# Second mixture of experts: up products in seven block products instead of eight, down products added up in SBUF

## The chip, the cores and the metric

The kernel runs on one core of one Trainium2 chip. The metric is the time of one execution on the device, in microseconds. Before the change it is 1548.05 us, the median of three runs (1547.43 to 1549.74). Smaller is better.

The names of the engines in what follows: PE is TensorE (matrix products), PEld its loads of stationary operands, DVE is VectorE, ACT is ScalarE, POOL is GpSimd, SP is SyncE (it issues the DMAs).

## The reference

Three stages follow each other. A clustered attention gives `x` (1536 tokens by 512), a first MoE block maps `x` to a new `x`, and the second MoE block, the one that changes, sums eight experts over all tokens:

```python
def _moe2_ref(x, w_gate, w1, w2):          # x 1536x512, w1 8x512x1024, w2 8x1024x512
    logits = x @ w_gate
    logits = logits - logits.max()
    P = np.exp(logits)
    for _ in range(8):
        P /= P.sum(1, keepdims=True) + 1e-09
        P /= P.sum(0, keepdims=True) + 1e-09
        P *= N / E
    out = np.zeros((N, D), dtype=np.float32)
    for e in range(E):
        h = np.maximum(x @ w1[e], 0.0)     # "up": 1536x512 by 512x1024
        ye = h @ w2[e]                     # "down": 1536x1024 by 1024x512
        out += P[:, e:e + 1] * ye
    return out
```

The eight rounds on `P` (called the gates here) need sums over all tokens and are a long chain of small steps. They are needed before an expert's result can be weighted and added, not before the up and down products.

## The kernel before

**Precision.** Every fp32 operand of a large product is kept as two parts, `hi` (rounded to fp32r) and `lo` (the rest). One product is three matmuls, `hi*lo + lo*hi + hi*hi`, all into the same PSUM bank: the helper `three` at L675, whose matmuls have the lines L677, L678 and L679 wherever it is called from. Making a pair costs an ACT copy (the `hi`) and a subtraction, on POOL for weights and on DVE for activations.

**Order.** The program is written in the order in which it runs: each engine works through its own queue in program order, and semaphores hold an instruction until what it needs is there. The attention and the first MoE are ordered by a planner; the second MoE is a plain loop at the end of the file, after `mixed` (the first MoE) has run out.

**Second MoE.** A unit `u` is one expert `e`, one block `blk` of 512 tokens (three blocks) and one tile `f` of 128 of the 1024 hidden columns (eight tiles): 8 x 3 x 8 = 192 units. `up(u)` runs 4 x 3 matmuls of 128x128 weights on 512 tokens into a bank of PSUM (name `l1_...`), then ACT takes the relu as the `hi` of `h` (L924) and DVE the rest (L925). `down(u)`, two units later (`LAG = 2`), runs for each of the four token tiles of the block three matmuls of 512 columns: here `h` is the stationary operand and `w2` streams. The four result banks `l2[t]` stay open over all eight tiles `f`, so that PSUM does the addition over the hidden columns; only after the eighth tile DVE weights the bank with the gate and adds it to `acc` (L946; L941 and L944 for the first expert). That is 96 evictions in all. Banks: four for `up` and the small products of the gates (`bank`, two pools of two), four for `l2`.

**Weights.** `fetch_w` brings 512 KB pieces (two tiles of `f`) into one of two buffers `wraw`, `load_w` splits them into `wh` (ACT, L840) and `wl` (POOL, L841); an expert's weights stay in SBUF for its 24 units and are replaced during its last block.

**Gates.** `gates()` is a generator of twelve small steps. A step ends with a small product on PE, and the next step's DVE operations read its result. One step is drawn between `up(u)` and `down(u - 2)`, so that a step's PE product stands in PE's queue one unit behind the DVE operations that it needs.

Of the kernel before, what the change touches and what calls it, by code (L numbers as in the profile page):

```python
# [8 lines left out]
F32 = mybir.dt.float32  # L9
# [128 lines left out]
def moe_kernel(ctx: ExitStack, tc: tile.TileContext, qk, nat, cen, wt, w123, wout, wgate, w1, w2, out):  # L138
# [536 lines left out]
    def three(ps, whi, wlo, xhi, xlo, first, last):  # L675

        nc.tensor.matmul(ps, whi, xlo, start=first, stop=False)  # L677
        nc.tensor.matmul(ps, wlo, xhi, start=False, stop=False)  # L678
        nc.tensor.matmul(ps, whi, xhi, start=False, stop=last)  # L679
# [137 lines left out]
    pools["w", 0] = ctx.enter_context(tc.tile_pool(name="w1_p", bufs=1, reuse_waits="tile"))  # L817
# [6 lines left out]
    wts = {}  # L824
    w_raw = {}
    PAIRS = NF2 // 2

    def fetch_w(e, m, p):
        if e < E:
            raw = pools["w", 0].tile([P, 2, DM], F32, tag="wraw", bufs=2, name=f"wraw{e}_{m}_{p}")  # L830
            nc.sync.dma_start(raw, (w1, w2)[m][e, :, p])
            w_raw[e, m, p] = raw

    def load_w(e, m, p):
        if e < E:
            raw = w_raw.pop((e, m, p))
            for j in range(2):
                hi = pools["w", m].tile([P, DM], F32R, tag="wh", bufs=NF2, name=f"wh{e}_{m}_{p}_{j}")
                lo = pools["w", m].tile([P, DM], F32R, tag="wl", bufs=NF2, name=f"wl{e}_{m}_{p}_{j}")
                nc.scalar.copy(hi, raw[:, j])  # L840
                nc.gpsimd.tensor_sub(lo, raw[:, j], f32(hi))  # L841
                wts[e, m, 2 * p + j] = hi, lo

    todo = [(0, m, p) for m in range(2) for p in range(PAIRS)]
    fetch_w(*todo[0])
    fetch_w(*todo[1])
    for n, _ in enumerate(mixed):
        if n % 40 == 20 and todo[0][1] == 0:
            load_w(*todo.pop(0))
            fetch_w(*todo[1])  # L850
    hctx.close()
    mctx.close()
    pools["w", 1] = ctx.enter_context(tc.tile_pool(name="w2_p", bufs=1, reuse_waits="tile"))
    e_p = ctx.enter_context(tc.tile_pool(name="e_p", bufs=1, reuse_waits="tile"))

    acc = [e_p.tile([P, DM], F32, tag="acc", bufs=NT, name=f"acc{t}") for t in range(NT)]


    def gates():
# [47 lines left out]
        for t in range(TPB):  # L907
            nc.vector.tensor_scalar(acc[t], acc[t], prob[:, t, :1], None, op0=ALU.mult)


    hts = {}
    l2 = {}
    units = [(e, blk, f) for e in range(E) for blk in range(NB) for f in range(NF2)]

    def up(u):
        e, blk, f = units[u]
        hi, lo = (w.rearrange("p (d f) -> p d f", f=P) for w in wts[e, 0, f])
        ts = slice(blk * TM, (blk + 1) * TM)
# [105 lines left out]
```

## Time and profile before

| | |
|---|---|
| median of three runs | 1548.05 us |
| profiled execution | 1547.56 us, of which 1545.7 us are its span (first to last instruction) |
| second MoE in it | from 491.8 us to the last matmul at 1541.5 us, then evictions and the last DMAs |
| busy in the span | PE 97%, DVE 35%, ACT 29%, POOL 32% |
| granted TensorE clock | 0.997 over the span, 1.00 over the second MoE |

The time of the profiled execution is 1.9 us more than its span, for what lies around the instructions. PE's busy share says that some matmul is under way, not that the array streams at its best: matmuls overlap their neighbours, so the pace is read from start to start. An engine's share over the span is a mean over three stages; for the change the second MoE alone counts.

### The profile page before, as it was taken

To read this page: it belongs to the slowest core of one execution; us is meant where nothing else is said; L and a number is where in the kernel's file an instruction comes from. 1 tells how busy PE (TensorE), PEld (TensorE's weight loads), DVE (VectorE), ACT (ScalarE), POOL (GpSimd) and SP (SyncE) were. 2 spreads that over 40 slices of the span, in tenths; PEclk is the share of its full clock that TensorE was granted. 3 is DMA by queue.
4 is the path that set the end of the run, shared out by engine and by line. 5 is a ranking of instruction groups with operands and counts; after the bars stand their busy time and mean duration, and the time that the engine had idled before them with its cause. 6 is when DMAs were issued, how large, how long until landed. Compare 5 with 4: busy or idle time off the path is not lost.

```text
span 1545.7 us, 18332 instructions
## 1 busy us (share of the span) xinstructions
PE 1504.5 (97%) x7304; PEld 1264.0 (82%) x7304; DVE 546.9 (35%) x994; ACT 448.0 (29%) x850; POOL 499.1 (32%) x491
## 2 busy tenths in 40 slices
PE   4999999899999999999999999999999999999999
PEld 3899998688877888888888888888888888888887
DVE  5899998545552331111121111111111111111111
ACT  3888888222222112211211211221131121112110
POOL 4899987756652002201400310230050022013000
PEclk9999999899999999999999999999999999999999
DMA  6554531222220001100300210020020011001000
GB/s 179 163 154 120 152 88 38 85 85 69 75 62 28 28 0 53 57 0 5 105 0 1 70 39 1 28 82 1 0 92 18 0 55 55 0 26 57 28 28 28
DMA packets 32132, 83.29 MB, mean 54 GB/s; under 512 B 4560, under 2 KB 9904, under 8 KB 32048
## 3 DMA queue, kind: packets, MB, share of 16 engines
q1 hardware_dynamic: 32048, 82.13, 18.0%
q8 instruction: 57, 0.93, 0.2%
q14 instruction: 27, 0.22, 0.0%
HBM read 65.55 MB, written 3.19 MB: 44 GB/s over the span
## 4 chain that ended last, share of the span: by engine, by line
PE 89%; POOL 5%; DVE 3%; ACT 2%; issue 1%; DMA 0%; POOLq 0%; DVEq 0%; ACTq 0%
PE l L677 23%; PE l L679 22%; PE l L678 22%; PE m L678 3%; PE m L679 3%; PE m L677 3%; PE y L491 3%; PE t L468 2%; PE s L430 2%; PE s L433 1%; PE mo L678 1%; PE mo L679 1%; PE mo L677 1%; POOL at L236 1%; PE sim L311 1%
## 5 line engine op out<-in xcount | busy, mean ns | idle before, releaser
L925 DVE SCALAR_TENSOR_TENSOR h<-l,h 128x512 fp32r<-128x512 f32 x192 | 132.8, 692 | 834.0 <-ACT h L924 834.0
L841 POOL TENSOR_TENSOR wl<-wraw,wh 128x512 fp32r<-128x512 f32 x128 | 162.2, 1300 | 801.1 <-ACT wh L840 801.1
L924 ACT ACTIVATE h<-l 128x512 fp32r<-128x512 f32 x192 | 114.9, 598 | 839.3 <-PE l L679 839.3
L677 PE MATMUL l<-wl,h 128*128 128x512 f32 x768 | 300.5, 391 | 0.0
L679 PE MATMUL l<-wh,h 128*128 128x512 f32 x768 | 299.3, 390 | 0.0
L679 PE MATMUL l<-x,wh 128*128 128x512 f32 x768 | 299.2, 390 | 0.0
L678 PE MATMUL l<-x,wl 128*128 128x512 f32 x768 | 299.2, 390 | 0.0
L678 PE MATMUL l<-wh,h 128*128 128x512 f32 x768 | 299.1, 389 | 0.0
L677 PE MATMUL l<-x,wh 128*128 128x512 f32 x768 | 299.1, 389 | 0.0
L679 PEld LDWEIGHTS l<-x,wh 128*128 128x128 f32 x768 | 144.3, 188 | 30.1
L679 PEld LDWEIGHTS l<-wh,h 128*128 128x128 f32 x768 | 144.2, 188 | 30.1
L677 PEld LDWEIGHTS l<-x,wh 128*128 128x128 f32 x768 | 144.2, 188 | 30.0
L678 PEld LDWEIGHTS l<-wh,h 128*128 128x128 f32 x768 | 144.3, 188 | 29.6
L677 PEld LDWEIGHTS l<-wl,h 128*128 128x128 f32 x768 | 144.3, 188 | 29.7
L678 PEld LDWEIGHTS l<-x,wl 128*128 128x128 f32 x768 | 144.2, 188 | 29.8
L444 DVE TENSOR_SCALAR_CACHE_REDUCE e<-s 128x768 f32<-128x768 f32 x96 | 92.6, 965 | 17.8 <-PE s L433 16.8
L452 ACT ACTIVATE e<-e,nm 128x768 f32<-128x768 f32 x96 | 90.1, 939 | 18.5 <-DVE e L444 18.1
L491 PE MATMUL y<-at,v 128*128 128x256 f32 x576 | 90.7, 295 | 2.9 <-POOL at L236 1.3
L678 PE MATMUL m<-x,mlo 128*128 128x512 f32 x216 | 86.0, 398 | 3.6 <-POOL mlo L671 3.6
L677 PE MATMUL m<-x,mhi 128*128 128x512 f32 x216 | 85.9, 398 | 0.0
L679 PE MATMUL m<-x,mhi 128*128 128x512 f32 x216 | 85.8, 397 | 0.0
L468 PE MATMUL t<-ident,e 128*128 128x128 f32 x576 | 81.1, 278 | 4.5 <-ACT e L452 2.2
(143 smaller groups left out, 1627.7 us busy)
## 6 DMA issues: line engine op xcount, KB each, us to landing
wraw<-in_w SPq DMA_DIRECT2D x64, 512.0 KB
mraw<-in_w SPq DMA_DIRECT2D x18, 512.0 KB
nat<-in_nat SPq DMA_DIRECT2D x16, 384.0 KB
raw<-in_qk SPq DMA_DIRECT2D x16, 384.0 KB
natv<-in_nat SPq DMA_DIRECT2D x16, 192.0 KB
r<-row SPq DMA_DIRECT2D x16, 192.0 KB
mraw<-in_wout SPq DMA_DIRECT2D x8, 384.0 KB
out<-acc SPq DMA_DIRECT2D x12, 256.0 KB
```

Source lines behind the costliest of these rows:

```text
L236: (nc.vector if engine == DVE else nc.gpsimd).tensor_sub(dst, a, b)
L430: nc.tensor.matmul(s()[:, c, :TB], sb()[:, qs], mb()[:, ks], start=True, stop=False)
L444: lambda e: nc.vector.tensor_scalar(ex(), scores(), -SCALE, None, op0=ALU.mult, op1=ALU.min, accum_out=nm()),
L452: lambda e: nc.scalar.activation(ex(), ex(), AF.Exp, bias=nm(), scale=-1.0, accum_out=sm()[:, n]),
L468: nc.tensor.transpose(t()[:, c, ks], ex()[:, c, ks], ident)
L491: nc.tensor.matmul(y(), v()[:, k], at()[:, l, :, k // 3, k % 3 * P : (k % 3 + 1) * P], start=n == 0, stop=n == 2 * NQ - 1)
L677: nc.tensor.matmul(ps, whi, xlo, start=first, stop=False)
L678: nc.tensor.matmul(ps, wlo, xhi, start=False, stop=False)
L679: nc.tensor.matmul(ps, whi, xhi, start=False, stop=last)
L841: nc.gpsimd.tensor_sub(lo, raw[:, j], f32(hi))
L924: nc.scalar.activation(h[:, 0], ps, AF.Relu)
L925: nc.vector.scalar_tensor_tensor(h[:, 1], ps, 0.0, f32(h[:, 0]), op0=ALU.max, op1=ALU.subtract)
```

## The change

A pair of hidden tiles (256 columns of one expert) becomes the unit of work: 32 pairs `n`. Tokens are halved (2 x 768), the 512 inputs are halved (2 x 256), and the pair's columns are its two tiles (2 x 128). So the up product of a pair is a 2x2 block product. It is now formed from seven products of block sums (Strassen's scheme in Winograd's form) instead of eight plain block products. The sums on the token side, `s1` to `s4`, are made once during pair 0, which itself still uses eight plain products (`up_blocks`). `s1` overwrites the block `a21` of `x2`. The sums on the weight side, `t1` to `t4`, are made for each pair on POOL.

The 768 tokens of a half don't fit one bank, so each product runs in two passes, of 512 and of 256 columns (`PASSES`). Partial results are combined on DVE (`u2`, `u3`, `c22`, `c21`, `c12`) or in PSUM: two of the banks `x`, `y`, `z`, `w` of a pass are written twice, the second product being added onto the first in place, which `skip_group_check` allows.

The down products of a pair are added up in PSUM over its two tiles only, and each of the twelve token tiles of each pair is then added to `acc` on DVE: 384 evictions instead of 96 (the twelve of pair 0 are ACT copies). Their order among the up products is written out in the strings `WAYS` (`u` one up product, `d` one token tile of a down product). `wraw` has three buffers instead of two. A gate step is drawn after each `u` of pair 0 and after every second `u` of pairs 1 to 3; up to six items of the generator `sum_blocks` are drawn after every step.

```diff
-    def three(ps, whi, wlo, xhi, xlo, first, last):
+    def three(ps, whi, wlo, xhi, xlo, first, last, more=False):
...
+    HALF = N // 2
+    PASSES = [(0, TM), (TM, HALF - TM)]
     PAIRS = NF2 // 2
...
+            use = ("b11", "t2", "b21", "t3", "t1", "t4", "b22")
+            ts = pools["w1"].tile([P, 4, 2 * P], F32, tag="ts", bufs=1, name=f"ts{n}")
+            src.update((f"t{k + 1}", ts[:, k]) for k in range(4))
+            for t, a, b in (("t1", "b12", "b11"), ("t2", "b22", "t1"), ("t3", "b22", "b12"), ("t4", "t2", "b21")):
+                nc.gpsimd.tensor_sub(src[t], src[a], src[b])
+            yield
+        for key in use:
+            w = wop[n, key] = pools["w1"].tile([P, 2, 2 * P], F32R, tag="wop", bufs=10, name=f"wop{n}_{key}")
+            nc.scalar.copy(w[:, 0], src[key])
+            nc.gpsimd.tensor_sub(w[:, 1], src[key], f32(w[:, 0]))
+            yield
...
+    def sum_blocks():
+        for o, n in PASSES:
+            for k in range(2):
+                v = {}
+
+                def made(key, fn, *args):
+                    v[key] = tmp(f"{key}_{o}_{k}", n)
+                    fn(v[key], *args)
+
+                for key in ("a21", "a22", "a11", "a12"):
+                    made(key, nc.vector.tensor_add, *map(f32, operand(key, k, o, n)))
+                    yield
+                made("s1", nc.vector.tensor_add, v["a21"], v["a22"])
+                yield
+                made("s3", nc.vector.tensor_sub, v["a11"], v["a21"])
+                yield
+                made("s2", nc.vector.tensor_sub, v["s1"], v["a11"])
+                yield
+                made("s4", nc.vector.tensor_sub, v["a12"], v["s2"])
+                yield
+                for key in ("s2", "s3", "s4", "s1"):
+                    hi, lo = operand(key, k, o, n)
+                    nc.scalar.copy(hi, v[key])
+                    nc.gpsimd.tensor_sub(lo, v[key], f32(hi))
+                    yield
+
+    def product(ps, n, key, xkey, o, c, first):
+        for k in range(2):
+            w = wop[n, key][:, :, k * P : (k + 1) * P]
+            hi, lo = operand(xkey, k, o, c)
+            three(ps, w[:, 0], w[:, 1], hi, lo, first and k == 0, k == 1, not first)
...
+    def up_products(n, i):
+        o, c = PASSES[i]
+        x, y, z, w = (bank([P, TM], f"{t}{n}_{i}")[:, :c] for t in "xyzw")
+        a, u2, u3, c22, c21, c12 = (tmp(f"{t}{n}_{i}", c) for t in ("a", "u2_", "u3_", "c22_", "c21_", "c12_"))
+        product(x, n, "b11", "a11", o, c, True)
+        nc.scalar.copy(a, x)
+        yield
+        product(y, n, "t2", "s2", o, c, True)
+        nc.vector.tensor_add(u2, y, a)
+        yield
+        product(x, n, "b21", "a12", o, c, False)
+        relu(h_tile(n, i, "11", c), x)
+        yield
+        product(y, n, "t3", "s3", o, c, False)
+        nc.vector.tensor_add(u3, y, a)
+        yield
+        product(z, n, "t1", "s1", o, c, True)
+        nc.vector.tensor_add(c22, z, u3)
+        relu(h_tile(n, i, "22", c), c22)
+        yield
+        product(w, n, "t4", "a22", o, c, True)
+        nc.vector.tensor_sub(c21, u3, w)
+        relu(h_tile(n, i, "21", c), c21)
+        yield
+        product(z, n, "b22", "s4", o, c, False)
+        nc.vector.tensor_add(c12, z, u2)
+        relu(h_tile(n, i, "12", c), c12)
+        yield
+
+    def down(n, i):
+        e, p = seq[n]
+        o, c = PASSES[i]
+        for r in (1, 0):
+            for t in range(c // P):
+                ts = slice(t * P, (t + 1) * P)
+                l2 = pools["l2"].tile([P, DM], F32, tag="l2", name=f"l2_{n}_{r}_{o}_{t}")
+                for j in range(2):
+                    h, w = hs[n, i, f"{r + 1}{j + 1}"], wdn[n, j]
+                    three(l2, h[:, 0, ts], h[:, 1, ts], w[:, 0], w[:, 1], j == 0, j == 1)
...
+    WAYS = {(0, 0): "uuuu", (0, 1): "uudddudddudd", 0: "uuduuduudud", 1: "uuddudududududd"}
```

Three places show how this stands in the engines' queues. The first is DVE during the gate rounds. Before, in units 6 and 7 of the first expert: `h` is an activation's low part, `c`, `rs`, `rse`, `rr` and `prob` belong to one gate round, whose operations follow each other.

```order
L925 SCALAR_TENSOR_TENSOR h_5676<-l_5_5663,h_5676 128x512
L899 TENSOR_REDUCE c_5680<-cs_5650 128x8
L901 TENSOR_SCALAR c_5682<-c_5680 128x8
L903 RECIPROCAL c_5684<-c_5682 128x8
L904 SCALAR_TENSOR_TENSOR prob<-prob,c_5684 128x96
L889 TENSOR_REDUCE rs_5687<-prob 128x12
L891 TENSOR_SCALAR rse_5689<-rs_5687 128x12
L893 RECIPROCAL rr_5691<-rse_5689 128x12
L894 TENSOR_TENSOR prob<-prob,rr_5691 128x96
```

After, in pair 0: `a_512_0` and `s_512_0` (L953) are items of `sum_blocks`, whose inputs all lie in SBUF.

```order
L930 SCALAR_TENSOR_TENSOR prob<-prob,c_5652 128x96
L915 TENSOR_REDUCE rs_5655<-prob 128x12
L917 TENSOR_SCALAR rse_5657<-rs_5655 128x12
L919 RECIPROCAL rr_5659<-rse_5657 128x12
L920 TENSOR_TENSOR prob<-prob,rr_5659 128x96
L953 TENSOR_TENSOR a_512_0_5663<-x_0_5071 128x256
L953 TENSOR_TENSOR a_512_0_5665<-x_2_5263 128x256
L953 TENSOR_TENSOR a_512_0_5667<-x_0_5071 128x256
L953 TENSOR_TENSOR a_512_0_5669<-x_2_5263 128x256
L953 TENSOR_TENSOR s_512_0_5671<-a_512_0_5663,a_512_0_5665 128x256
L953 TENSOR_TENSOR s_512_0_5673<-a_512_0_5667,a_512_0_5663 128x256
L986 SCALAR_TENSOR_TENSOR h_1_22_5688<-z_1_22_5675,h_1_22_5688 128x256
```

Between one gate round and the next, DVE's queue now holds up to six additions of blocks beside the one operation on `h`.

The second is PE at the same place. Before, the product `cs` of a gate round stands between the twelve matmuls of an `up` and those of a `down`:

```order
L678 MATMUL l_5_5663<-x_3_5371,wl_0_2_1_4503 128x512
L679 MATMUL l_5_5663<-x_3_5371,wh_0_2_1_4503 128x512
L897 MATMUL cs_5650<-prob,ones 128x96
L677 MATMUL l_0_0_5567<-wl_1_1_1_5494,h_5604 128x512
L678 MATMUL l_0_0_5567<-wh_1_1_1_5493,h_5604 128x512
```

After, in pair 0 (`z_1_21` and `z_1_22` are plain block products of the second pass):

```order
L678 MATMUL z_1_21_5628<-x_3_5345,wop_b_4285 128x256
L679 MATMUL z_1_21_5628<-x_3_5345,wop_b_4285 128x256
L923 MATMUL cs_5615<-prob,ones 128x96
L677 MATMUL z_1_22_5675<-x_0_5071,wop_b_4487 128x256
L678 MATMUL z_1_22_5675<-x_0_5071,wop_b_4487 128x256
```

The product `cs` now follows a product of twelve matmuls of 256 columns, and the matmuls behind it in PE's queue are up products too.

The third is DVE in a later pair. Before, deep in an expert: low parts of `h`, and now and then four evictions into `acc`.

```order
L925 SCALAR_TENSOR_TENSOR h_8988<-l_104_8975,h_8988 128x512
L925 SCALAR_TENSOR_TENSOR h_9016<-l_105_9003,h_9016 128x512
L946 SCALAR_TENSOR_TENSOR acc_5451<-l_96_0_8819,prob,acc_5451 128x512
L946 SCALAR_TENSOR_TENSOR acc_5452<-l_96_1_8823,prob,acc_5452 128x512
L946 SCALAR_TENSOR_TENSOR acc_5453<-l_96_2_8827,prob,acc_5453 128x512
L946 SCALAR_TENSOR_TENSOR acc_5454<-l_96_3_8831,prob,acc_5454 128x512
L925 SCALAR_TENSOR_TENSOR h_9048<-l_106_9035,h_9048 128x512
```

After, most of the first pass of pair 6:

```order
L1046 SCALAR_TENSOR_TENSOR acc_5438<-l_5_1_512_0_7350,prob,acc_5438 128x512
L986 SCALAR_TENSOR_TENSOR h_0_11_7364<-x_0_7318,h_0_11_7364 128x512
L1011 TENSOR_TENSOR u_6_0_7324<-y_0_7319,a_0_7322 128x512
L1046 SCALAR_TENSOR_TENSOR acc_5439<-l_5_1_512_1_7377,prob,acc_5439 128x512
L1014 TENSOR_TENSOR c_6_0_7325<-z_0_7320,u_6_0_7324 128x512
L986 SCALAR_TENSOR_TENSOR h_0_22_7392<-c_6_0_7325,h_0_22_7392 128x512
L1018 TENSOR_TENSOR c_6_0_7326<-u_6_0_7324,w_0_7321 128x512
L986 SCALAR_TENSOR_TENSOR h_0_21_7402<-c_6_0_7326,h_0_21_7402 128x512
L1046 SCALAR_TENSOR_TENSOR acc_5432<-l_5_0_512_0_7408,prob,acc_5432 128x512
L1022 TENSOR_TENSOR c_6_0_7327<-z_0_7320,u_6_0_7323 128x512
L986 SCALAR_TENSOR_TENSOR h_0_12_7423<-c_6_0_7327,h_0_12_7423 128x512
L1046 SCALAR_TENSOR_TENSOR acc_5433<-l_5_0_512_1_7426,prob,acc_5433 128x512
```

DVE's queue has gained the combinations of the block products (`u`, `c`) and four times the evictions, and an operation on `h` stands behind the combination that it waits for.

## Rows read from the trace of the kernel before

**Rows 1.** Page, parts 1 and 4: busy us; shares of the last chain.

```profile
PE 1504.5 (97%) x7304; PEld 1264.0 (82%) x7304; DVE 546.9 (35%) x994; ACT 448.0 (29%) x850; POOL 499.1 (32%) x491
...
PE 89%; POOL 5%; DVE 3%; ACT 2%; issue 1%; DMA 0%; POOLq 0%; DVEq 0%; ACTq 0%
```

**Rows 2.** Busy us by stretch: length, PE, PEld, DVE, ACT, POOL; clock, DMA share.

```profile
491.70:1541.90 1050.20, 1050.20 (x4646) 868.56 (x4645) 209.01 (x356) 183.51 (x319) 151.46 (x120) 1.00 0.10 32
1100.00:1132.70 32.70, 32.70 (x146) 27.10 (x145) 6.79 (x10) 6.63 (x12) 5.33 (x5) 1.00 0.10 33
```

**Rows 3.** Timeline of PE in the second MoE: start us, us, what.

```profile
699.91 0.39 PE L677 MATMUL l<-x,wh 128*128 128x512 f32 x1
...
702.63 0.39 PE L677 MATMUL l<-wl,h 128*128 128x512 f32 x1
```

**Rows 4.** Timeline of PE, attention, matmuls of 256 columns.

```profile
161.06 0.88 PE L491 MATMUL y<-at,v 128*128 128x256 f32 x6
```

**Rows 5.** The same matmuls and their weight loads, groups by line and form.

```profile
L491 PE MATMUL y<-at,v 128*128 128x256 f32 x576 | 90.7, 295 | 2.9 <-POOL at L236 1.3 <-DVE x L508 1.0 <-POOL rr L407 0.3
L491 PEld LDWEIGHTS y<-at,v 128*128 128x128 f32 x576 | 79.4, 195 | 5.3 <-POOL at L236 1.8 <-issue 1.6 <-POOL rr L407 0.6
```

**Rows 6.** Groups by form, whole span: busy us, mean ns | idle before, releaser.

```profile
L841 POOL TENSOR_TENSOR wl<-wraw,wh 128x512 fp32r<-128x512 f32 x128 | 162.2, 1300 | 801.1 <-ACT wh L840 801.1
L925 DVE SCALAR_TENSOR_TENSOR h<-l,h 128x512 fp32r<-128x512 f32 x192 | 132.8, 692 | 834.0 <-ACT h L924 834.0
L924 ACT ACTIVATE h<-l 128x512 fp32r<-128x512 f32 x192 | 114.9, 598 | 839.3 <-PE l L679 839.3
L840 ACT CAST wh<-wraw 128x512 fp32r<-128x512 f32 x128 | 72.8, 619 | 18.4 <-PE l L679 17.9 <-DMA wraw<-in_w 0.5
L946 DVE SCALAR_TENSOR_TENSOR acc<-l,prob,acc 128x512 f32<-128x512 f32 x84 | 57.1, 743 | 4.8 <-PE l L679 4.8
```

**Rows 7.** Groups by form from 302 to 490 us, pieces of 384 columns.

```profile
L671 POOL TENSOR_TENSOR mlo<-ma,mt 128x384 fp32r<-128x384 f32 x8 | 8.1, 1011 | 1.6 <-DVE mt L667 1.1
L667 DVE SCALAR_TENSOR_TENSOR mt<-mraw,mt 128x384 f32<-128x384 uint32 x8 | 4.5, 556 | 0.2
```

**Rows 8.** Timeline of DVE in one round of the gates.

```profile
521.02 0.25 DVE L899 TENSOR_REDUCE c<-cs 128x8 f32<-128x96 f32 x1
...
522.79 0.26 DVE L894 TENSOR_TENSOR prob<-prob,rr 128x96 f32<-128x96 f32 x1
```

**Rows 9.** Timeline of DVE from 329 to 343 us.

```profile
329.49 0.69 DVE L661 SCALAR_TENSOR_TENSOR ma<-mraw,mt 128x512 int32<-128x512 int32 x1
330.22 0.43 DVE L665 TENSOR_SCALAR mt<-ma 128x512 int32<-128x512 int32 x1
...
339.06 0.98 DVE L661 SCALAR_TENSOR_TENSOR ma<-mraw,mt 128x512 int32<-128x512 int32 x1
340.07 1.42 DVE L665 TENSOR_SCALAR mt<-ma 128x512 int32<-128x512 int32 x1
341.52 0.69 DVE L667 SCALAR_TENSOR_TENSOR mt<-mraw,mt 128x512 f32<-128x512 uint32 x1
```

**Rows 10.** Timeline of POOL at the same time.

```profile
339.59 1.62 POOL L733 TENSOR_TENSOR ht<-mt,ht 128x512 fp32r<-128x512 f32 x1
341.63 1.73 POOL L669 TENSOR_TENSOR ma<-ma,mhi 128x512 f32<-128x512 f32 x1 [0.43 <-DVE mt L665]
```

**Rows 11.** Timeline of PE after a wait (in brackets) before the first MoE.

```profile
290.19 0.50 PE L678 MATMUL m<-x,mlo 128*128 128x512 f32 x1 [3.64 <-POOL mlo L671]
...
291.87 0.63 PE L677 MATMUL m<-x,mhi 128*128 128x512 f32 x1
292.30 0.63 PE L678 MATMUL m<-x,mlo 128*128 128x512 f32 x1
```

**Rows 12.** Timeline of PE in the first MoE.

```profile
399.64 0.39 PE L678 MATMUL m<-x,mlo 128*128 128x512 f32 x1
...
402.44 0.39 PE L678 MATMUL m<-x,mlo 128*128 128x512 f32 x1
```

More of the change, by code (lines that the diff above doesn't have):

```diff
@@ L928, in down @@
-    def down(u):
-        e, blk, f = units[u]
-        hi, lo = wts[e, 1, f]
-        h = hts.pop(u)
-        for t in range(TPB):
-            if f == 0:
-                l2[t] = pools["l2"].tile([P, DM], F32, tag="l2", name=f"l2_{u}_{t}")
-            ts = slice(t * P, (t + 1) * P)
-            three(l2[t], h[:, 0, ts], h[:, 1, ts], hi, lo, f == 0, f == NF2 - 1)
-            if f == NF2 - 1:
-                tt = blk * TPB + t
-                if e == 0 and blk == 0:
-                    nc.scalar.copy(acc[tt], l2[t])
+    half = lambda d, h, o, n: [x2[d][:, l, h * HALF + o : h * HALF + o + n] for l in range(2)]
@@ new lines, in moe_kernel, with operand @@
+    sums = {k: [s_p.tile([P, 2, HALF], F32R, tag=f"s{k}_{d}", name=f"s{k}_{d}") for d in range(2)] for k in (2, 3, 4)}
+    def operand(key, k, o, n):
+        if key in ("a11", "a12", "a21", "a22"):
+            return half(2 * (int(key[2]) - 1) + k, int(key[1]) - 1, o, n)
+        if key == "s1":
+            return half(k, 1, o, n)
+        return [sums[int(key[1])][k][:, l, o : o + n] for l in range(2)]
+    def sum_blocks():
[21 more added lines that the diff above has]
+                    yield
@@ new lines, in moe_kernel @@
+    later = iter(())
+    WAYS = {(0, 0): "uuuu", (0, 1): "uudddudddudd", 0: "uuduuduudud", 1: "uuddudududududd"}
+    for n in range(len(seq)):
+        for i in range(2):
+            if i == 0:
+                fetch_w(1, n + 1)
+                fetch_w(0, n + 2)
+                if n == 0:
+                    for _ in down_weights(0):
+                        pass
+                ahead_w = up_weights(n + 1)
+                ahead_d = down_weights(n + 1)
+            ups = up_products(n, i) if n else up_blocks(n, i)
+            k = 0
+            for step in WAYS[(0, i) if n == 0 else i]:
+                if step == "d":
+                    next(later)
+                else:
+                    next(ups)
+                    if i == 0 and (n == 0 or k in (0, 1, 3, 5)) or i == 1 and k < 4:
+                        next(ahead_w, None)
+                    if i == 1 and k >= (2 if n == 0 else 4):
+                        next(ahead_d, None)
+                    if seq[n][0] == 0 and (k % 2 == 1 or n == 0):
+                        next(gate, None)
+                    k += 1
+                for _ in range(6):
+                    next(blocks, None)
+            assert next(later, None) is None and next(ups, None) is None
+            later = down(n, i)
@@ L980 @@
+    for _ in later:
+        pass
 def kernel(q, k, v, centroids, moe_w1, moe_w2, moe_w3, moe_w_out, moe2_w_gate, moe2_w1, moe2_w2):
```

140 lines of the change are left out of this document (66 added, 74 removed).

## Prediction

> **What bounds the kernel now.** I read the page first: PE is busy for 1504.5 of 1545.7 us, and PE makes up 89% of the chain that ended last [rows 1]. Then the busy time by stretch: in the second MoE PE never rests, its clock is granted in full (2.4 GHz), and DVE, ACT and POOL are busy for 6.8, 6.6 and 5.3 us in a piece of 32.7 us [rows 2]. So there the time is the number of matmuls times their pace, and the other engines have room. The timeline of PE gives the pace: twelve matmuls of 512 columns start between 699.91 and 702.63, which is 0.2267 us each [rows 3]. The stage's 4608 matmuls make 1044.6 us of its 1050.2 [rows 2]; the other 5.6 us are the small products of the gates, and they stay. The question is therefore what PE's queue holds afterwards, and whether PE ever waits in it.
>
> **The steady pairs.** Before, a pair of hidden tiles has 72 up and 72 down matmuls of 512 columns: 144 x 0.2267 = 32.64 us. After, seven products of two input blocks and three matmuls each make 42 matmuls per pass, one pass of 512 and one of 256 columns; the down part keeps its 72. A matmul of 256 columns stands in the attention: six take 0.88 us, and one alone about 0.295, so they start (0.88 - 0.295)/5 = 0.117 us apart [rows 4, 5]. I take 0.12, since the stream that is cut in two pays its fixed part twice: half of 0.2267 would be 0.113. A pair then costs 42 x 0.12 + (42 + 72) x 0.2267 = 5.04 + 25.84 = 30.88 us, 1.76 us less, and 31 pairs save **54.6 us**. Pair 0 still forms eight products, in two passes: 48 x 0.12 + 48 x 0.2267 + 72 x 0.2267 = 32.96 us, **0.3 us** more than before.
>
> The Trainium skill (TensorE: Matmul & The Clock Gate, section Back-to-back issue gap) puts the gap at columns over 2.4 GHz plus 2.5 ns, so 0.216 us for 512 and 0.109 us for 256 columns; by that the pairs would save 58.6 us. The rows are slower on both, 0.2267 and 0.117 us, and the sum goes by the rows.
>
> What must lie beside this: per pair DVE gets 12 evictions at 0.743, and 9 operations (five combinations, four low parts of `h`) in each pass, at 0.69 for 512 columns [rows 6]. For 256 columns I go down a line from 512 to 384 columns (0.69 to 0.556 us [rows 7]) to 0.42. That is 8.9 + 6.2 + 3.8 = 18.9 us of 30.9. POOL gets four sums and seven low parts of weights of 256 columns at 0.72 (1.30 and 1.011 us at 512 and 384 [rows 6, 7]) and two of 512: 10.5 us. ACT gets 5 copies or relus of 0.60 and at most the same again for the short pass, and 9 weight copies of at most 0.62: under 11.6 us [rows 6]. No engine is near PE's 30.9.
>
> Totals don't exclude waits, so I followed the queues. A low part of `h` on DVE stands behind its combination and waits for ACT's relu between the two; behind it in DVE's queue stand the evictions that free a result bank. In the short pass one `u` and one `d` take PE 6 x 0.12 + 6 x 0.2267 = 2.08 us, and DVE needs 0.42 + 0.60 (ACT, at most) + 0.42 + 0.74 = 2.18. Three such steps leave DVE 0.3 us late, and the two `d` and two `u` that follow without a combination repay it; four result banks give PE 5.4 us of patience. `h` of the last product is needed two to four steps later, 4 us or more against a chain of 2.2 us. In-place accumulation (`x`, `y`, `z`) waits for a read that began at least two steps before. I put the steady waits at zero; a wait of 1 us per pair would be 31 us (a rival below). The DMAs are as many as before, 512 KB each, at a DMA share of 0.10 [rows 2], and a third `wraw` buffer lets SP issue them a pair ahead: nothing.
>
> **The start, pair 0.** Here DVE gets 32 additions of blocks whose two inputs both lie in SBUF, 16 of 512 and 16 of 256 columns: 16 x 0.69 + 16 x 0.42 = 17.8 us. Beside them POOL has eight low parts of 512 columns and 17 operations of 256 (eight low parts, four weight sums, five low parts of weights): 8 x 1.30 + 17 x 0.72 = 22.6 us. The trace shows what such work does to its neighbour. DVE's operation with two SBUF inputs takes 0.69 us at 329.49 with POOL idle and 0.98 at 339.06, and its single-input neighbour 0.43 and 1.42, each time while POOL works; POOL's subtraction, 1.30 us as a rule, takes 1.73 when it meets 0.69 us of DVE at 341.5 [rows 9, 10]. DVE operations that read PSUM don't show this (0.692 in the mean of 192 [rows 6]). So in pair 0 the two queues largely take turns.
>
> That reaches PE through the gates. DVE's queue holds up to six of these additions between one gate round and the next, and PE's `cs` product waits for the round. If the two engines excluded each other wholly, 17.8 + 22.6 = 40.4 us would begin when the first `h` is done (2.7 + 0.60 + 0.69 = 4.0 us into the stage) and end at 44.4; the last `h` and gate round of the pair (0.42 + 2.0, from 521.02 to 523.05 before [rows 8]) let the last `cs` go at 46.8, and two `d` (2.7) end PE's queue of pair 0 at 49.5. Its own work there is 16.6 (up) + 10.9 (eight `d`) + 1.4 (logits) + 0.6 (transposes, gate products) = 29.5. So PE would wait for 20 us. The 341.63 row says less: POOL grew by 0.43 of DVE's 0.69, so 0.26 us of each meeting overlaps, and 32 meetings give 8.3 us back: 12 us. With no exclusion DVE's own queue (17.8, low parts of `h` 4.4, four rounds 8.0) is as long as PE's, and its turns with PE would still cost some 5 us; with every meeting lost and the tile ring of the sums (eight buffers, freed by POOL) holding DVE as well, 25. I take **15 us**, between the two readings of the rows, and keep 5 and 25. No wait like this exists before: PE is busy throughout the stage [rows 2].
>
> The Trainium skill (SBUF — State Buffer, section Who interferes with whom) calls the shared port of DVE and POOL an exclusive lock, taken by a DVE instruction with two SBUF inputs against a POOL instruction that reads SBUF, the second blocking until the first ends. By that rule the start costs the 20 us, and the time would be 1516; the row of 1.73 us shows a shorter loss than a full block, which is why I stay lower.
>
> Two smaller terms hang on it. After a PE wait of 3.64 us matmuls of 512 columns started 0.43 us apart, at the lower clock level (1.2 GHz), for about eight matmuls [rows 11]: 8 x 0.2 = **1.6 us**, once. Four gate rounds are left for pair 1, one per two `u`, with 4.1 us of PE between them against 2.0 us of round and about 2.2 us of DVE's other work: **1 us**.
>
> **Sum.** -54.6 + 0.3 + 15 + 1.6 + 1 = -36.7 us from the profiled 1547.6: **1511 us**. The median of the runs is 0.5 us above the profiled execution, which changes nothing here.
>
> **Rivals.**
> 1. *Weight loads set the pace of the short pass; slower.* Each matmul has its own load of 128 columns, whose record lasts 0.195 us, and the 576 matmuls of 256 columns fill 90.7 us, 0.157 each [rows 5]. The new kernel has 42 x 31 = 1302 of them. At 0.19 us they cost 1302 x 0.07 = 91 us more: 1602. It decides from 0.12 + 36.7/1302 = 0.148 us on. Against it: six such matmuls with full loads in 0.88 us [rows 4], so loads overlap; the 0.157 includes the ends of short groups.
> 2. *PE falls back to the pace of the first MoE.* There twelve matmuls of the same shape take 2.80 us, 0.2333 each, at the same granted clock [rows 12]. I don't know why the second MoE is 3% faster; it has calmer neighbours [rows 2], and the change makes them busier. 114 x 31 x 0.0066 = 23 us: 1534.
> 3. *The start costs little*, because PE's need comes earlier than the end of the sums and POOL runs ahead: 5 us and no fall of the clock: 1499.
> 4. *The steady pairs wait*, DVE's chain of combination, relu and low part falling behind: 1 us per pair gives 1542, and from 1.2 us per pair on nothing is gained. For it: 18.9 us of DVE work with ACT in its middle. Against it: the slack counted above.
>
> **How the numbers follow.** Forecast 0.62 (1501 to 1521), rival 3 0.12 (1492 to 1501), rival 2 0.13 (1521 to 1540), rival 4 0.07 (1521 to 1565), rival 1 0.06. The range 1492 to 1537 holds the forecast, rival 3 and most of rival 2. Runs of this kernel lie within 0.15% of each other, so a change of 0.2% (3.1 us) can be told from none. Faster: the forecast, rivals 2 and 3 and half of rival 4, 0.90. Slower: rival 1 and the worst of rival 4, 0.07. The rest, 0.03, is no change.
>
> **What would show it.** In the profile after, steady pairs should repeat every 30.9 us with PE free of waits; 256-column matmuls 0.12 us apart and 512-column ones 0.2267. Pair 0 should last about 45 us, with PE's waits in front of `cs`, and L953 on DVE and the subtractions on POOL longer than 0.69 and 1.30 us. DVE should be busy for about 19 us per pair. The forecast is wrong if the first two rows of the sum (pace and repeats) differ, if PE's waits lie in the steady pairs, or if pair 0 runs through.

## Result and the profile after

The changed kernel takes 1522.33 us in the median (1521.34 to 1522.88), the kernel before beside it 1547.74: a ratio of 0.9834, 95% interval 0.9817 to 0.9851. The forecast was 1511, with a range of 1492 to 1537. The time fell by 25 us where 36.7 had been forecast.

The page of the profile after, to be laid beside [rows 1]: busy us of each engine, and the shares of the chain that ended last.

```profile
PE 1466.4 (96%) x7700; PEld 1250.5 (82%) x7700; DVE 963.2 (63%) x1688; ACT 541.1 (36%) x1157; POOL 696.3 (46%) x788
...
PE 87%; POOL 5%; DVE 4%; ACT 2%; issue 2%; DMA 0%; POOLq 0%; DVEq 0%; ACTq 0%
```

PE lost 38 us of work and DVE gained 416, but the chain still runs through PE. The answer to [rows 2] is a table of four stretches, with the same columns. They are pair 0 from its first `z` to the first `x` of pair 1, the two pieces of it in which the clock was halved, and one steady pair.

```profile
491.99:543.64 51.65, 37.39 (x174) 30.21 (x173) 39.31 (x81) 19.32 (x45) 33.76 (x35) 0.83 0.10 31
512.83:526.49 13.66, 7.22 (x24) 6.25 (x25) 10.90 (x30) 3.81 (x9) 6.35 (x6) 0.50 0.00 0
540.14:543.55 3.41, 3.41 (x10) 2.64 (x9) 1.99 (x6) 0.59 (x1) 2.67 (x4) 0.50 0.83 279
1105.91:1137.08 31.17, 31.17 (x157) 26.41 (x156) 18.58 (x30) 8.42 (x19) 10.82 (x14) 1.00 0.12 35
```

In pair 0 PE rests for 51.65 - 37.39 = 14.3 us, and twice it works at 1.2 GHz (granted clock 0.50). In the steady pair it never rests, though the pair takes 31.17 us where 30.88 had been forecast. From its first matmul to the end of its last the second MoE went from 1050.1 us (491.77 to 1541.91) to 1025.0 (491.99 to 1516.95), which is the whole difference between the two profiled executions (1547.56 and 1522.45 us).

PE's timeline in pair 0 (start us, us, what; in brackets the idle time before it and what ended it) has these four waits and no other.

```profile
506.82 0.38 PE L909 MATMUL gbc<-gm,ones 1*128 1x1 f32 x2 [1.07 <-DVE gm L906]
...
515.52 0.74 PE L923 MATMUL cs<-prob,ones 128*128 128x96 f32 x2 [6.70 <-DVE prob L920]
...
522.62 0.74 PE L923 MATMUL cs<-prob,ones 128*128 128x96 f32 x2 [3.75 <-DVE prob L920]
...
539.00 0.43 PE L923 MATMUL cs<-prob,ones 128*128 128x96 f32 x2 [2.73 <-DVE prob L920]
```

All stand in front of products of the gates. Ahead of the longest, DVE's queue held additions of blocks. These are DVE's groups of them from 500 to 556 us (busy us, mean ns of one); the first four of 512 columns, at 496.18, took 0.93 us in the mean.

```profile
L953 DVE TENSOR_TENSOR a<-x 128x512 f32<-128x512 f32 x4 | 5.4, 1417 | 0.0
L953 DVE TENSOR_TENSOR a<-x 128x256 f32<-128x256 f32 x8 | 5.0, 684 | 0.0
```

And POOL's groups of the subtractions of the sums (`lo`) in the same stretch:

```profile
L969 POOL TENSOR_TENSOR s<-s,s 128x512 fp32r<-128x512 f32 x6 | 7.5, 1277 | 8.2 <-ACT s L968 8.2
...
L969 POOL TENSOR_TENSOR x<-s,x 128x512 fp32r<-128x512 f32 x2 | 3.0, 1506 | 0.0
```

An addition that costs 0.69 us alone takes 1.42. Six of POOL's eight subtractions keep their 1.30 us [rows 6], but most of those had no addition beside them. Where the two kinds meet, both get longer:

```profile
506.70 5.44 DVE L953 TENSOR_TENSOR a<-x 128x512 f32<-128x512 f32 x4
...
507.59 1.74 POOL L969 TENSOR_TENSOR x<-s,x 128x512 fp32r<-128x512 f32 x1
509.29 1.17 POOL L853 TENSOR_TENSOR wop_t<-ts,wop_t 128x256 fp32r<-128x256 f32 x1
```

Each of these two operations of POOL, and the next, takes 0.44 us more than without DVE beside it (1.30 and 0.73), each of DVE's four 0.5 to 1.1 us more than 0.68. They take turns: by the trace's nanoseconds each of the four additions ends 0.55 us after the operation of POOL beside it.

Before the other three waits DVE itself had rested, for 2.02, 1.73 and 1.63 us. The gate round stood behind a low part of `h` that waited for ACT's relu (L985), and the relu stood behind the copies of sums (L968), which wait for DVE's additions. For the third wait:

```profile
516.10 1.66 ACT L968 CAST s<-s 128x512 fp32r<-128x512 f32 x3 [1.69 <-DVE s L953]
...
518.59 0.42 DVE L986 SCALAR_TENSOR_TENSOR h<-z,h 128x256 fp32r<-128x256 f32 x1 [1.73 <-ACT h L985]
```

The rounds ahead of the third and fourth wait then took 3.6 us, beside POOL's operations, where [rows 8] show 2.0.

The steady pairs' pace stands in the starts of PE's matmuls. An up product (into `x`, `y`, `z` or `w`) and a down group (into `l`, a `d` of the order) are six matmuls each; a few groups' first starts are enough.

```profile
1103.17 0.40 PE L677 MATMUL l<-w,h 128*128 128x512 f32 x1
...
1104.56 0.39 PE L677 MATMUL l<-w,h 128*128 128x512 f32 x1
...
1105.91 0.39 PE L677 MATMUL x<-x,wop_b 128*128 128x512 f32 x1
...
1108.64 0.39 PE L677 MATMUL l<-w,h 128*128 128x512 f32 x1
...
1110.04 0.39 PE L677 MATMUL x<-x,wop_b 128*128 128x512 f32 x1
...
1121.06 0.28 PE L677 MATMUL x<-x,wop_b 128*128 128x256 f32 x1
...
1121.77 0.28 PE L677 MATMUL y<-s,wop_t 128*128 128x256 f32 x1
...
1137.09 0.39 PE L677 MATMUL x<-x,wop_b 128*128 128x512 f32 x1
```

Six matmuls of 256 columns take 0.71 us, 0.119 each. The `d` at 1103.17, right behind an up product, takes 1.39 us for six; the next one, behind a `d`, 1.36 to a rounding, which is the pace of [rows 3]. The `d` of the first pass at 1108.64 takes 1.40. From `x` at 1105.91 to `x` at 1137.09 is the pair. Taken to the nanosecond, each pair has six `d` at 1.387, four at 1.401 and two at 1.360: 6 x 0.027 + 4 x 0.041 = 0.33 us over twelve clean ones, less 42 x 0.0012 that the short products gain on 0.12, and 0.02 more in the long up products that follow a `d`. That is the 0.29 us.

### The profile page after: what moved, and what is told of

Read it like the earlier page. It is cut to its first block, busy times and chain, and to the rows that moved or that the text cites. A ratio compares the mean times of both kernels' runs of the same rounds, so it can differ in the third digit from the quotient of the medians.

```text
span 1520.7 us, 20558 instructions
## 1 busy us (share of the span) xinstructions
PE 1466.4 (96%) x7700; PEld 1250.5 (82%) x7700; DVE 963.2 (63%) x1688; ACT 541.1 (36%) x1157; POOL 696.3 (46%) x788
## 4 chain that ended last, share of the span: by engine, by line
PE 87%; POOL 5%; DVE 4%; ACT 2%; issue 2%; DMA 0%; POOLq 0%; DVEq 0%; ACTq 0%
PE l L677 12%; PE l L678 12%; PE l L679 11%; PE m L678 3%; PE m L677 3%; PE m L679 3%; PE z L679 3%; PE z L677 3%; PE z L678 3%; PE y L679 3%; PE x L678 3%; PE y L678 3%; PE x L679 3%; PE y L677 3%; PE x L677 3%; PE y L491 3%
## 5 line engine op out<-in xcount | busy, mean ns | idle before, releaser
L1046 DVE SCALAR_TENSOR_TENSOR acc<-l,prob,acc 128x512 f32<-128x512 f32 x336 | 251.6, 749 | 127.4 <-PE l L679 124.3
L677 PE MATMUL l<-w,h 128*128 128x512 f32 x768 | 305.0, 397 | 0.0
L678 PE MATMUL l<-w,h 128*128 128x512 f32 x768 | 303.5, 395 | 0.0
L679 PE MATMUL l<-w,h 128*128 128x512 f32 x768 | 302.0, 393 | 0.0
L985 ACT ACTIVATE h<-c 128x512 fp32r<-128x512 f32 (+1 forms) x186 | 97.7, 525 | 364.4 <-DVE c L1014 188.1
L853 POOL TENSOR_TENSOR wop_t<-ts,wop_t 128x256 fp32r<-128x256 f32 x124 | 90.7, 741 | 257.5 <-ACT wop_t L852 192.5
L853 POOL TENSOR_TENSOR wop_b<-wraw,wop_b 128x256 fp32r<-128x256 f32 x97 | 78.9, 813 | 260.6 <-ACT wop_b L852 260.6
L986 DVE SCALAR_TENSOR_TENSOR h<-c,h 128x512 fp32r<-128x512 f32 (+1 forms) x186 | 111.2, 598 | 113.9 <-ACT h L985 113.9
L679 PEld LDWEIGHTS l<-w,h 128*128 128x128 f32 x768 | 145.1, 189 | 33.6
L677 PEld LDWEIGHTS l<-w,h 128*128 128x128 f32 x768 | 145.7, 190 | 25.5
L678 PEld LDWEIGHTS l<-w,h 128*128 128x128 f32 x768 | 145.7, 190 | 24.5
L863 POOL TENSOR_TENSOR w<-wraw,w 128x512 fp32r<-128x512 f32 x64 | 82.8, 1294 | 118.4 <-ACT w L862 118.4
L985 ACT ACTIVATE h<-x 128x512 fp32r<-128x512 f32 (+1 forms) x62 | 30.4, 491 | 196.1 <-PE x L679 196.1
L491 PEld LDWEIGHTS y<-at,v 128*128 128x128 f32 x576 | 79.5, 195 | 5.2 <-POOL at L236 1.6
L679 PE MATMUL y<-s,wop_t 128*128 128x512 f32 (+1 forms) x248 | 83.4, 336 | 0.0
```

The lines of the kernel that those rows point to most:

```text
L491: nc.tensor.matmul(y(), v()[:, k], at()[:, l, :, k // 3, k % 3 * P : (k % 3 + 1) * P], start=n == 0, stop=n == 2 * NQ - 1)
L677: nc.tensor.matmul(ps, whi, xlo, start=first, stop=False, skip_group_check=more)
L678: nc.tensor.matmul(ps, wlo, xhi, start=False, stop=False, skip_group_check=more)
L679: nc.tensor.matmul(ps, whi, xhi, start=False, stop=last, skip_group_check=more)
L853: nc.gpsimd.tensor_sub(w[:, 1], src[key], f32(w[:, 0]))
L863: nc.gpsimd.tensor_sub(w[:, 1], raw[:, j], f32(w[:, 0]))
```

## Experiments

Two questions: why the start costs what it does, and why the down groups are slow. Tiles' start addresses below are those that the allocator gave, modulo 128 bytes: 32 for the weights of both parts, for `x` and the sums, and for `h` of the first pass, 0 for `h` of the second; 96 for the first MoE's weights.

**Gate rounds after pair 0.**

```
-                    if seq[n][0] == 0 and (k % 2 == 1 or n == 0):
+                    if seq[n][0] == 0 and (k % 2 == 1 if n else i == 0 and k < 3):
```

> Of the gate steps only the first three stay in pair 0 (the logits, the transposes, the maximum); the other rounds run in the pairs after it, one for every two up products. Theory A, PE waits because a gate round stands behind the additions of the block sums in DVE's queue: without rounds in pair 0 the three waits in front of cs there (7.0, 4.2 and 3.0 us) and both falls of the clock go, pair 0 falls from 51.7 us to 31 to 34, and the time from 1522 to about 1503. Theory B, the sums themselves are late (DVE and POOL get in each other's way for the 44 us that full exclusion gives): pair 1 then waits for s2, s3, s1 and s4 instead, and pair 0 and pair 1 together get shorter by less than 8 us: 1515 or more.

1511.83 us (ratio to before 0.9767, 0.9753 to 0.9782). Pair 0 fell from 51.65 to 42.90 us, pairs 0 and 1 together from 83.98 to 75.93. So half of theory A: the waits for `cs` are gone, one other came. PE's waits in that stretch (engine, line waited for: us, times, longest):

```profile
PE l L677 <- ACT acc L1038: 10.1, 1, 10.1
```

ACT's copies of finished down products stand in its queue behind the copies of sums (L968), which wait for DVE's additions; PE then has no free result bank. And an effect that nobody asked for: the edit moved `h` of the second pass to 96, and a steady pair fell from 31.173 to 31.053 us.

**Low parts of the sums on DVE.**

```
-                    nc.gpsimd.tensor_sub(lo, v[key], f32(hi))
+                    nc.vector.tensor_sub(lo, v[key], f32(hi))
```

> The low parts of the block sums (8 of 512 and 8 of 256 columns) go from POOL to DVE; the gate rounds stay in pair 0. Theory A, DVE and POOL shut each other out in pair 0, so that the sum of both engines' work counts: 10.4 + 5.8 us leave POOL and 5.5 + 3.4 come to DVE, the sum falls by 7 us and pair 0 goes from 51.7 to about 45. Theory B, only the length of DVE's queue ahead of a gate round counts: 8.9 us come to it and pair 0 goes to about 60, the time to 1531.

1516.16 us (0.9802, 0.9785 to 0.9818); pair 0 took 44.84 us where theory A said 45 and B 60. DVE has 16 operations more and is done earlier. Its groups from 500 to 556 us, as above:

```profile
L953 DVE TENSOR_TENSOR a<-x 128x256 f32<-128x256 f32 x8 | 2.8, 418 | 0.0
...
L953 DVE TENSOR_TENSOR a<-x 128x512 f32<-128x512 f32 x4 | 2.5, 672 | 0.0
```

The additions went from 1.417 to 0.672 and from 0.684 to 0.418 us: what had held them was POOL's subtractions. The waits for `cs` did not all go: 3.73, 3.33 and 0.66 us of them are left.

**Sums three steps at a time.** As the first experiment, and

```
-                for _ in range(6):
+                for _ in range(3):
                     next(blocks, None)
```

> As the first experiment (gate rounds after pair 0), and the block sums are issued three steps at a time instead of six, over all of pair 0's 16 places. Theory A, PE waits because low parts of h and the copies of down products stand behind additions in the in-order queues of DVE and ACT: with half as many ahead of each the wait of 10.1 us goes to under 2 us, pair 0 falls from 42.9 to 31 to 34 us and the time from 1512 to about 1502. Theory B, the sums need the 40 us however they are spread: the wait moves to the first products of pair 1 that read them, and the time stays within 3 us of 1512.

1508.93 us (0.9758, 0.9739 to 0.9777). Pair 0 fell to 31.44 us, as A said, and pair 1 rose to 41.15, as B said; together 72.59, 3.3 less than with six. The time, 2.9 us below the first experiment's, is what B said. PE's waits:

```profile
PE x L677 <- ACT a L1002: 6.3, 1, 6.3
PE l L677 <- ACT acc L1038: 0.9, 1, 0.9
```

ACT's timeline there:

```profile
532.14 0.40 ACT L968 CAST s<-s 128x256 fp32r<-128x256 f32 x1 [2.73 <-DVE s L953]
...
533.85 0.58 ACT L1002 COPY a<-x 128x512 f32<-128x512 f32 x1
```

The copy of `x`, which pair 1 needs at once, is again queued behind the last copies of sums, which it does not need before its second pass.

**Tiles of `h` at other addresses.** Thirty-two bytes ahead of `h` of the second pass, which starts at 32 then:

```
+        e_p.tile([P, 8], F32, tag="pad", bufs=1, name="pad")
         lg = e_p.tile([P, NT, E], F32, tag="lg", bufs=1, name="lg")
```

> Thirty-two bytes of nothing are allotted ahead of the tiles of h of the second pass, so that these start at 32 bytes past a multiple of 128, as the first pass's tiles of h, the weights, x and the sums do, and not at a multiple of 128. Theory A, where a 128-column weight load starts in SBUF sets the pace of the matmuls: the four down groups per pair that read these tiles, at 1.401 us for six matmuls, go to about 1.36, a pair from 31.17 to about 31.0, and the time falls by about 4.7 us. Theory B, the slower pace comes from what precedes the group (up products) or from the other engines' traffic: nothing changes, 31.17 and 1522.

1521.82 us (0.9831, 0.9817 to 0.9846) and a pair of 31.173: theory A fell. The four groups went from 1.401 to 1.397 only, and the up groups around them gave that back. One of the four, between up products of 512 columns, with every tile at 32:

```profile
1108.52 0.40 PE L677 MATMUL l<-w,h 128*128 128x512 f32 x1
...
1109.92 0.39 PE L677 MATMUL x<-x,wop_b 128*128 128x512 f32 x1
```

The same tile ahead of all of `h`:

```
+    e_p.tile([P, 8], F32, tag="pad", bufs=1, name="pad")
     def tmp(name, n):
```

> The tiles of h of the first pass start at 64 bytes past a multiple of 128 (they stood at 32), those of the second at 32 (they stood at 0). Theory A, the start address of h sets how slow a down group behind up products is (1.401 us with h of the second pass at 0, 1.397 at 32, 1.374 at 96): the groups of pass 1, at 1.387, change by 0.01 us or more, and those of pass 0 stay at 1.397. Theory B, the address has nothing to do with it: 1.387 stays and a pair takes 31.17 us.

One run, 1525.63 us, a pair of 31.293. PE's starts at the end of the second pass:

```profile
1104.79 0.39 PE L677 MATMUL l<-w,h 128*128 128x512 f32 x1
...
1106.18 0.40 PE L677 MATMUL l<-w,h 128*128 128x512 f32 x1
...
1107.58 0.39 PE L677 MATMUL x<-x,wop_b 128*128 128x512 f32 x1
```

The `d` behind a `d`, 1.36 us so far, takes 1.40 with `h` at 64, and no longer recovers. So the address does count, but not by the simple rule of theory A.

**The first MoE's weights moved by 64 bytes**, from 96 to 32:

```
                 nc.scalar.copy(best[n], ps)
+                if (f, n) == (0, NB - 1):
+                    m_p.tile([P, 16], F32, tag="pad", bufs=1, name="m_pad")
```

> Sixty-four bytes of nothing are allotted among the tiles of the first MoE, so that its weight tiles start at 32 bytes past a multiple of 128 and not at 96. Theory A, the start address of the weight loads sets the pace: the first MoE's matmuls go from 0.2333 to 0.2267 us each and the time falls by some 5 us or more. Theory B, the first MoE is 3% slower because of its busier neighbours (DVE, ACT, POOL): 0.2333 stays and the time is 1522.

1515.89 us (0.9794, 0.9779 to 0.9808), 6.4 less than the changed kernel. PE's starts in the first MoE, the answer to [rows 12], twelve matmuls apart:

```profile
399.71 0.39 PE L679 MATMUL m<-x,mhi 128*128 128x512 f32 x1
...
402.43 0.39 PE L679 MATMUL m<-x,mhi 128*128 128x512 f32 x1
```

2.72 us, 0.2267 each: theory A. Only buffers of the weight path moved (the raw, temporary and finished weight tiles and the running maxima); PE reads the finished ones alone.

**Eight products, the rest of the change kept.**

```
-    blocks = sum_blocks()
+    blocks = iter(())
...
-    WAYS = {(0, 0): "uuuu", (0, 1): "uudddudddudd", 0: "uuduuduudud", 1: "uuddudududududd"}
+    WAYS = {(0, 0): "uuuu", (0, 1): "uudddudddudd", 0: "uududdud", 1: "uudddudddudd"}
...
-            ups = up_products(n, i) if n else up_blocks(n, i)
+            ups = up_blocks(n, i)
```

The sums `t1` to `t4` of the weights are left out too, and the weights are split at other steps.

> The other parts of the change without the seven products: every pair forms its eight products of blocks, in two passes of 512 and 256 columns, and adds its down products to SBUF as the changed kernel does; there are no block sums. Theory A, the gain is the products': a pair costs 48 x (0.119 + 0.227) + 72 x 0.227 = 32.95 us, up to 33.3 if the down groups behind up products are as slow as now, pair 0 has no sums in its way, and the time is 1549 to 1562, not below before. Theory B, part of the gain lies in the new order or in the down part: a pair below 32.64 us, and the time below 1545.

1567.86 us (1.0129, 1.0114 to 1.0144), slower than before. A pair takes 33.20 us, inside theory A's 32.95 to 33.3; the total that I had put beside it was too low (31 x 0.56 = 17 us over the 1547.34 beside it, and 3 more in the rest). PE's starts in it:

```profile
1100.58 0.39 PE L677 MATMUL l<-w,h 128*128 128x512 f32 x1
...
1101.98 0.40 PE L677 MATMUL l<-w,h 128*128 128x512 f32 x1
...
1103.38 0.40 PE L677 MATMUL z<-x,wop_b 128*128 128x512 f32 x1
...
1110.38 0.40 PE L677 MATMUL l<-w,h 128*128 128x512 f32 x1
...
1111.77 0.39 PE L677 MATMUL l<-w,h 128*128 128x512 f32 x1
...
1113.13 0.39 PE L677 MATMUL l<-w,h 128*128 128x512 f32 x1
```

With `h` of the second pass (at 0) both `d` in a row take 1.40; with that of the first (at 32) the first takes 1.39 and the next 1.36. The seven products are worth 33.20 - 31.17 = 2.03 us a pair, each version with its own order of `u` and `d`, and the cut into two passes and its order cost 0.56.

**Up products computed and dropped** (`PLAIN` lists the seven products in their order).

```
+        if n > 1:
+            for t, key, xkey, f in PLAIN:
+                product({"x": x, "y": y, "z": z, "w": w}[t], n, key, xkey, o, c, f)
+                yield
+            return
...
-                    h, w = hs[n, i, f"{r + 1}{j + 1}"], wdn[n, j]
+                    h, w = hs[min(n, 1), i, f"{r + 1}{j + 1}"], wdn[n, j]
```

> From pair 2 on the up products are computed and not used: no combinations, no relu, no low parts, and the down products read the tiles of h of pair 1 (same addresses). PE's instructions and their order are the same. Theory A, the slower down groups behind up products (1.387 and 1.401 us against 1.360) come from DVE and ACT reading and writing SBUF while they finish an up product: the groups go to 1.360 and a pair from 31.17 to about 30.88. Theory B, they come from PE's own change from the operands of up to those of down: nothing changes, 31.17.

One run, 1525.21 us, with a second MoE that began 4.3 us later (at 496.32), ahead of the edit. A steady pair still takes 31.173 us, to the nanosecond: theory B. Busy times from 700 to 1200 us, first of the changed kernel, then of this one:

```profile
700.00:1200.00 500.00, 500.00 (x2503) 423.57 (x2502) 298.05 (x482) 134.71 (x304) 174.44 (x211) 1.00 0.11 35
```

```profile
700.00:1200.00 500.00, 500.00 (x2506) 423.67 (x2505) 144.93 (x193) 62.84 (x146) 166.73 (x211) 1.00 0.11 35
```

DVE and ACT do half of their work, and PE's starts are as before (1.39, then 1.36):

```profile
1105.93 0.40 PE L677 MATMUL l<-w,h 128*128 128x512 f32 x1
...
1107.32 0.39 PE L677 MATMUL l<-w,h 128*128 128x512 f32 x1
...
1108.68 0.39 PE L677 MATMUL x<-x,wop_b 128*128 128x512 f32 x1
```

So the slow groups don't come from what DVE and ACT do. POOL's work and the DMAs stayed nearly as they were and are not tested by this.

**All together, and longer runs of `u` and `d`.** The pad of the first MoE, gate rounds from pair 2 on, two steps of sums at a time, and

```
-    WAYS = {(0, 0): "uuuu", (0, 1): "uudddudddudd", 0: "uuduuduudud", 1: "uuddudududududd"}
+    WAYS = {(0, 0): "uuuu", (0, 1): "uudddudddudd", 0: "uuduuuduudd", 1: "uudduuuddduuddd"}
```

> Four edits together, told apart by the stage they touch: the pad that moves the first MoE's weight tiles (as in the fourth experiment, 6 us); gate rounds only from pair 2 on; block sums two steps at a time, so that those of the second pass are made in pair 1; and up and down products in longer runs (seven places in a pair where down follows up, instead of ten). Theory A on the start, PE waits only because too many sums stand ahead of its evictions in the in-order queues: pair 0 and pair 1 together, 72.6 us with three steps at a time, take 63 to 66. Theory B, the sums need their time however they are spread: 70 or more. Theory A on the down groups, every change of TensorE from up to down operands costs a fixed 0.014 (pass 0, h at 96) or 0.028 us (pass 1): a steady pair takes 31.053 - 0.014 - 3 x 0.028 = 30.95 us. Theory B, what counts is how many down groups there are: 31.05. With theory A twice the time is 1491 to 1496.

1499.67 us (0.9684, 0.9665 to 0.9702), above the 1491 to 1496 of the two theories A. Pairs 0 and 1 took 67.2 us, between the theories. A steady pair took 30.993: in the second pass three changes to `d` less save 3 x 0.028, and each change back, whose first short up matmul comes 0.007 us early, loses its gain: 31.053 - 3 x 0.021 = 30.99. In the first pass nothing was saved, as with `h` at 96 the second `d` in a row takes 1.374 too.

The same with the edit of the second experiment:

> The same with the low parts of the block sums on DVE instead of POOL. Theory A, DVE and POOL slow each other wherever both work from SBUF: pair 0 and pair 1 together are as short as or shorter than with POOL, by up to 3 us. Theory B, once the sums are thin the start has no waits left and DVE's 8.9 us more in its queue can only harm: equal or longer by up to 4 us.

1497.09 us (0.9664, 0.9646 to 0.9683), the fastest version: 52 us below the kernel before beside it (1549.06), 25 below the change. Theory A again: pairs 0 and 1 (the two rows) take 64.1 us, and PE waits for 2.2 of them.

```profile
485.97:516.24 30.27, 30.27 (x165) 25.06 (x163) 23.20 (x35) 15.26 (x33) 12.33 (x13) 1.00 0.06 18
516.24:550.09 33.85, 31.67 (x157) 26.19 (x156) 27.51 (x51) 14.73 (x36) 15.77 (x18) 1.00 0.18 54
```

**Two equal passes**, on that version, with a pad of 64 bytes ahead of `h` of the second pass:

```
-    PASSES = [(0, TM), (TM, HALF - TM)]
+    PASSES = [(0, HALF // 2), (HALF // 2, HALF // 2)]
```

> The version with the low parts on DVE, but with two passes of 384 columns instead of 512 and 256, all tiles of h at 32 bytes past a multiple of 128, and seven up and six down groups in each pass, three places per pass where down follows up. Theory A, any change from up to down operands disturbs the six matmuls that follow: the first down group after up products takes 1.38 to 1.40 us and the ones behind it 1.36. Theory B, only up matmuls of 256 columns, or h of the second pass, disturb it, as the kernel before has such changes too, with 512 columns on both sides, and no loss: all twelve down groups take 1.36. The 84 up matmuls are 0.173 to 0.176 us each by the rows of 384 columns in the attention, so a pair takes 30.9 to 31.2 us under B and 0.12 to 0.2 more under A; the time is within 6 us of 1497.

1505.62 us (0.9721, 0.9707 to 0.9735) and a pair of 31.28 us (two passes of 15.64). PE's starts:

```profile
1102.74 0.39 PE L677 MATMUL l<-w,h 128*128 128x512 f32 x1
...
1104.13 0.39 PE L677 MATMUL l<-w,h 128*128 128x512 f32 x1
...
1105.50 0.33 PE L677 MATMUL x<-x,wop_b 128*128 128x384 f32 x1
...
1106.57 0.33 PE L677 MATMUL y<-s,wop_t 128*128 128x384 f32 x1
...
1107.61 0.33 PE L677 MATMUL z<-x,wop_t 128*128 128x384 f32 x1
```

Theory A by the pair: with all tiles at 32 the first `d` takes 1.39, the second 1.37, and the first up group behind them 1.07 where the next takes 1.04. A change costs in both directions here. The time missed its bound: 8.5 us above 1497, where 6 had been allowed.

## Why the prediction was right or wrong

*Faster, and through PE alone*: right. The time came out 11.3 us above the forecast. By its own terms:

| term | forecast | measured |
|---|---|---|
| pairs 1 to 31 (54.6 less 1 for the gates of pair 1) | -53.6 | 30 x (31.173 - 32.64) + 32.33 - 32.64 = -44.3 |
| pair 0 (0.3 + 15 + 1.6), measured as what is left of the medians' difference | +16.9 | -25.4 + 44.3 = +18.9 |

*The steady pair's pace* is the term that failed, by 9.3 us. "42 x 0.12 + (42 + 72) x 0.2267" has the right count and the right price of the short matmuls (0.119) and of the long up ones. But the 0.2267 of [rows 3] was taken over for down groups that now stand between up products only six matmuls long. Ten of the twelve pay 0.027 or 0.041 us for that. It isn't the traffic of DVE and ACT (the dropped up products, 31.173 again); it goes with the change from the operands of up to those of down (three changes fewer in the longer runs saved 0.06 us a pair, and the equal passes show the loss too), and the start address of the weights that TensorE loads has a say in whether and how far the stream recovers (`h` at 64; the eight products). How a change of operands costs this, no run shows. Nor can I say why the kernel before has no such loss between its up and down parts, where all start at 32 and all have 512 columns: with the pad of 32 bytes the groups of the first pass had both as well, and lost 0.037 us each in going to `d`.

*Rival 2* named a fall to 0.2333, and gave it to busier neighbours. Four of the twelve down groups did run at that (1.401 for six), but the reason was wrong: 64 bytes took the first MoE to 0.2267 with the same neighbours, and halving the work of DVE and ACT in the second changed nothing.

*The start* was right in size, and in its mechanism in part: 15 us of PE's waits forecast, 14.3 measured, all in front of the gates' products, so that rival 3 (5 us) fell. Of these 6.7 stood behind additions in DVE's queue that POOL slows, as forecast. The other 7.6 the timelines put down to a path that the prediction doesn't have, ACT's queue, where relus stood behind the copies of sums, and to gate rounds of 3.6 us instead of 2.0; no run takes that path away by itself. That the sum came so near 15, a figure chosen between 12 and 20, is luck in part.

Two further details were wrong. The clock: "1.6 us, once" became two falls, with 7.22 + 3.41 us of PE's work at half speed, at most half of which, 5.3 us, is their price; 0.3 + 14.3 + 5.3 = 19.9 against 18.9 measured. (Pair 0 lasted 51.65 us and not about 45. Beside the clock, PE's own work in it had been counted some 2 us too short: 28.1 us without the logits, which lie ahead of the first `z`, where the fastest version, without waits there, takes 30.27.) And who gives way: from [rows 10] I let a meeting lengthen POOL alone, by 0.43 us; in pair 0 it lengthened POOL's operations by 0.44 and DVE's additions by 0.5 to 1.1 as well. The Trainium skill (SBUF — State Buffer, section Who interferes with whom) calls the port that DVE and POOL share an exclusive lock, contended by a DVE operation with two SBUF inputs and a POOL operation that reads SBUF. The turns that the two take from 506.70 us on, and the 1.417 us against 0.672 without POOL's subtractions, bear that out for single meetings better than my partial overlap did; my 20 us by that rule were too many since they let all 32 additions collide, and 12 of them were slowed.

*Weight loads* (rival 1) don't pace the short matmuls: 0.119 us with a load each. *Steady waits* (rival 4): none. DVE was forecast at 18.9 us a pair and took 18.58; POOL 10.5 and 10.82.

## What to carry to other kernels

A pace measured in one stream holds for that stream: where a change sets other matmuls side by side, price the groups behind each change of operands apart, and try a small pad ahead of the tiles that TensorE loads as weights, and measure it: of three tried alone, one gave 6.4 us, one nothing, and one cost 0.12 us a pair. One-time work that is spread over a stage should enter each in-order queue in small portions, since whatever stands behind a large one waits too: in ACT's queue as well as in DVE's. And it belongs on the engine that doesn't slow its neighbour, even where that one looks busier. Edits of these kinds, 6.4 us of them in the first MoE, gave 25 us together, as much as the change itself.

## What the runs showed that was not expected

- 64 bytes in the start of the weight tiles change the pace of a whole stage of 512-column matmuls: 0.2333 us at 96, 0.2267 at 32 (6.4 us of 1522). For the tiles of `h` a second `d` in a row takes 1.360 us at 32 (1.37 behind products of 384 columns), 1.374 at 96, 1.40 at 64 and at 0. That is four addresses and no rule.
- The matmuls settle into such a pace over six to twelve matmuls after a change of operands; 0.027 us there and -0.007 back with 256 columns, 0.03 and 0.01, then 0.025 back, with 384, and 0.037 there and 0.004 back with 512, all tiles at 32. The kernel before shows nothing of it.
- An addition of two SBUF operands on DVE, the mean of four, took 1.417 us beside POOL's subtractions and 0.672 without; 12 of the 32 additions of pair 0 were slowed.
